# Block-sparse attention with an FFN on one core: the prologue's copies, banks and first matmuls rearranged

## The chip, the cores and the metric

The kernel runs on one core of a Trainium2 chip. The metric is the device time of one execution in microseconds (us), lower is better. The core has five engines with queues of their own that work in order: PE (matmul, with its weight loads shown apart as PEld), DVE, ACT, POOL, and SP, which here only issues DMAs. ACT issues a few DMAs too.

## The reference

```python
B, H, S, D = 4, 8, 768, 64; block = 32; n_blocks = 24
scores = q @ k.T / sqrt(D)
mask = |blk_i - blk_j| <= 1, or first/last block row or column, or kb in sampled_blocks[qb] (3 each)
scores = where(mask, scores, -1e9); scores -= scores.max(-1)
attn = exp(scores); attn /= attn.sum(-1) + 1e-9
x = (attn @ v) laid out as (B*S, 512)
h = x @ w_in                          # 512 -> 2048
g = where(h >= 1, h, where(h <= -1, 0, (h + 1)**2 / 4))
out = g @ w_out                       # 2048 -> 512
```

## The kernel before

The kernel goes through 32 pairs of batch and head. The eight heads of batch 0 are walked twice, half the queries (384) at a time, so that the first of two FFN passes can start early: 40 visits, of which the first is called head 0 here, the second head 1, and so on.

**A visit** has two parts. First come the row maxima: `max_mm` multiplies a 128-query slice with 384 keys (K = 88 rows: 64 of the head's dimension and 24 of the mask), `max_red` takes the maximum of that product on DVE, `max_col` joins two halves, `max_turn` transposes three columns into a row by PE with the identity `idr`, and `max_row` (ACT) writes the negative row into row 96 of the query operand. Then come the scores proper (K = 97, the extra row subtracts the maximum), `expo` on ACT, and the products with the values. A visit of batch 0's first pass has six `max_mm`, six score tiles and six exponentials.

**The mask** is carried by extra rows of the matmul. `ind` is a matrix of 38 rows and 768 columns from DRAM: 24 rows say to which block a column belongs, 8 are zero, 6 are one. It lands three times: in a scratch tile `raw` (called `early["ef"]` in the code), and in rows 64 to 101 of the two key tiles `KF[0]` and `KF[1]`. `mask()` makes a 24 by 24 table `mb` on DVE from the constants `cmt` and the sampled blocks `sraw`; `mask_half` multiplies it with the indicator on PE and copies the product into rows 64 to 87 of `QA[0]`; `mask_copies` spreads it to the other query tiles.

**Raw heads.** Heads 0 and 1 (`RAW`) are loaded into `KF`, `QF` (named KB, QB in rows of the trace) and used in full fp32 for the scores. `round_raw` casts them to fp32r into `KA0`, `QA0` (KA, QA; `KAt`, `QA` in the code) for the maxima.

**Order.** All steps lie in a list `plan` with a due time from tables of numbers (`P`, `PW`, ...); it is sorted once and written out, so every engine's order is fixed. `consts` (-100), `load_raw` of head 0 (-99), `consts_more` (-98), `mask` (-97) come first. DMAs take eight semaphores in turn, so an issue on SP waits until the DMA eight places before it has landed.

**PSUM.** `bank` hands out banks by rings of names: `RINGS["m"]` holds the three buffers of the pool `pa`, from which the first maxima and their transposes come; `RINGS["s"]` (`oa0`, `oa1`, `hp`) serves the scores.

Of the kernel before, what the change touches and what calls it, by code (L numbers as in the profile page):

```python
# [10 lines left out]
I32 = mybir.dt.int32  # L11
# [7 lines left out]
B, H, S, D = 4, 8, 768, 64  # L19
NB, BLK, NR = 24, 32, 3  # L20
T = 6
HALF = 384
# [5 lines left out]
KM = 64 + NB  # L28
KA = 96 + T
# [9 lines left out]
def body(ctx, tc, qk_t, v, sampled_blocks, moe_w_in, moe_w_out, ind, cm, ident, fold, out):  # L39
    nc = tc.nc  # L40
# [12 lines left out]
    cv = pool("cv", 1)  # L53
# [19 lines left out]
    def f(ap):  # L73
        return ap.bitcast(F32)
# [7 lines left out]
    QA = [cst.tile([128, S], F32R, name=f"QA{i}") for i in range(SETS)]  # L82
    KAt = [cst.tile([128, S], F32R, name=f"KA{i}") for i in range(SETS)]
# [3 lines left out]
    KF = [f(qk.tile([128, S], F32R, name="KB")) for i in range(2)]  # L87
    QF = [f(qk.tile([128, S], F32R, name="QB"))[:, 0:HALF] for i in range(2)]
    RAWS = len(KF)
# [7 lines left out]
    M = slice(64, KM)  # L97
    early = {}

    def consts():  # L100
        ef = early["ef"] = f(cv.tile([128, 1024, 2], I32, name="raw", bufs=2).rearrange("p c w -> p (c w)"))[64:KA, 0:S]
        nc.scalar.dma_start(out=ef, in_=ind)
        sraw = early["sraw"] = cst.tile([128, NR, 2], I32, name="sraw")
        nc.sync.dma_start(out=sraw[M], in_=sampled_blocks.bitcast(I32).rearrange("a (r w) -> a r w", w=2))
        cmt = early["cmt"] = cst.tile([128, 2 * NB], F32, name="cmt")
        nc.sync.dma_start(out=cmt[M], in_=cm)
        nc.vector.memset(eps, 1e-9)
        nc.vector.memset(half_c, 0.5)
        nc.scalar.copy(out=warm, in_=eps)
        nc.gpsimd.memset(f(QA[0][64:128]), 0.0)  # L110
        nc.gpsimd.memset(QF[0][64:128], 0.0)
        for i in range(1, ALL):
            nc.gpsimd.memset(f(QA[i][64:96]), 0.0)

    def consts_more():
        idf = early["idf"] = pp.tile([128, HALF], F32, name="pt")[:, 0:128]
        nc.sync.dma_start(out=idf, in_=ident)
        nc.vector.tensor_copy(out=KAt[0][64:KA], in_=early["ef"])
        nc.scalar.dma_start(out=KF[0][64:KA], in_=ind)
        rounded(nc.gpsimd, KAt[1][64:KA], early["ef"])  # L120

    def mask():
        sf = cst.tile([128, NR], F32, name="sf")
        nc.vector.tensor_copy(out=sf[M], in_=early["sraw"][M, :, 0])
        al = cst.tile([128, NB], F32, name="al")
        cmt = early["cmt"]
        nc.vector.tensor_copy(out=al[M], in_=cmt[M, 0:NB])
        for r in range(NR):
            nc.vector.scalar_tensor_tensor(
                out=al[M], in0=cmt[M, NB:2 * NB], scalar=sf[M, r:r + 1], in1=al[M],  # L130
                op0=ALU.is_equal, op1=ALU.max)
        mb = early["mb"] = cst.tile([128, NB], F32R, name="mb")
        nc.vector.tensor_scalar(out=mb[M], in0=al[M], scalar1=-1.0, scalar2=BIG, op0=ALU.add, op1=ALU.mult)
        mask_half(0, nc.vector)

    def mask_half(hf, eng):
        cs = slice(hf * HALF, (hf + 1) * HALF)
        pm = psa.tile([128, 512], F32, name="pa")
        nc.tensor.matmul(out=pm[0:NB, 0:HALF], lhsT=early["mb"][M], rhs=KAt[0][64:KM, cs], start=True, stop=True)
        rounded(eng, QA[0][64:KM, cs], pm[0:NB, 0:HALF])  # L140
        if hf == 0:
            nc.scalar.copy(out=QF[0][64:KM], in_=pm[0:NB, 0:HALF])

    def mask_copies():
        src = f(QA[0][64:KM, 0:HALF])
        rounded(nc.gpsimd, QA[1][64:KM, 0:HALF], src)
        nc.scalar.copy(out=idr, in_=early["idf"])
        for i in range(1, RAWS):
            nc.gpsimd.memset(QF[i][64:96], 0.0)
            nc.scalar.dma_start(out=KF[i][64:KA], in_=ind)  # L150
            rounded(nc.gpsimd, QF[i][64:KM], src)
        rounded(nc.gpsimd, KAt[2][64:KA], f(KAt[0][64:KA]))
        rounded(nc.gpsimd, QA[2][64:KM, 0:HALF], src)
        nc.sync.dma_start(out=sel, in_=fold)
        for i in range(3):
            nc.gpsimd.memset(PS[i], 0.0)
        nc.gpsimd.memset(ones, 1.0)
# [9 lines left out]
    def after(key, *needs):  # L167
        assert all(x in passed for x in needs), (key, needs)
        passed.add(key)
# [34 lines left out]
    def bank(wide, use="s"):  # L204

        if wide:
            ring = RINGS[use]
            n = turns[use] = turns.get(use, -1) + 1
            name = ring[n % len(ring)]
            if name[0] == "o":  # L210
                return psc.tile([128, DM], F32, name=name)
            if name == "hp":
                return psh.tile([128, 512], F32, name="hp")
        return psa.tile([128, 512], F32, name="pa")
# [47 lines left out]
    L, R = slice(0, 64), slice(64, 128)  # L262

    def rounded(eng, dst, src):
        if eng is nc.vector:
            eng.tensor_copy(out=dst, in_=src)
        elif eng is nc.gpsimd:
            eng.tensor_scalar(out=dst, in0=src, scalar1=1.0, scalar2=0.0, op0=ALU.mult, op1=ALU.add)
        else:
            eng.copy(out=dst, in_=src)  # L270

    def end_of(n):
        return ("S", n, 0 if n < H else 1, T - 1)

    def visit(n, n0, b, h, hfs, pst):

        j, e = divmod(h, 2)
        wide = n < H
        raw = n in RAW
        unit = len(hfs) == 1  # L280
# [3 lines left out]
        m = n % ALL if unit else (n + 1) % SETS  # L284
        QAi, KAi = QA[m], KAt[m]
        qs = slice(hfs[0] * HALF, (hfs[-1] + 1) * HALF)
        st = {}

        def free():
            m = n - (ALL if n <= 2 * H else SETS)  # L290
            return [] if m < 0 else [("red", m, TH - 1, 1)] if m in RAW else [end_of(m)]

# [5 lines left out]
        def round_raw():  # L298
            after(("A", n), ("raw", n), *free())
            rounded(nc.scalar, KAi[L], KF[n % RAWS][L])  # L300
            rounded(nc.scalar, QAi[L, qs], QF[n % RAWS][L])

        def load_direct():
            after(("ld", n), *([("B", n - 2)] if n - 2 in DIRECT else []))
# [79 lines left out]
        def max_mm(t, kh):  # L384
            after(("mm", n, t, kh), ("A", n))
            if "mc" not in st:
                st["mc"] = pr.tile([128, T, 2], F32, name="mc", bufs=2)
            pm = bank(wide, "m")
            nc.tensor.matmul(out=pm[:, 0:HALF], lhsT=QAi[0:KM, t * 128:(t + 1) * 128],  # L389
                             rhs=KAi[0:KM, kh * HALF:(kh + 1) * HALF], start=True, stop=True)  # L390
            st["pm", t, kh] = pm
# [11 lines left out]
        def max_turn(hf):  # L403
            after(("turn", n, hf), ("col", n))
            pm = st["pr", hf] = bank(wide, "m")
            for t in range(TH):
                nc.tensor.transpose(out=pm[0:1, t * 128:(t + 1) * 128].bitcast(F32R),  # L407
                                    in_=st["mr"][:, hf * TH + t - t0:hf * TH + t + 1 - t0], identity=idr)
# [7 lines left out]
        for m, (t, kh) in enumerate(jobs):  # L416
            u = n0 - (G["m0"] - G["m1"] * m / len(jobs))
            at(u, max_mm, t, kh)
            at(u + G["mr"], max_red, t, kh)
        at(n0 - G["mc"], max_col)  # L420
        for hf in hfs:
            at(n0 - G["mt"], max_turn, hf)
            at(n0 - G["mw"], max_row, hf)
# [104 lines left out]
        w = HALF * len(hfs)  # L528
# [33 lines left out]
        s = n0  # L562
# [160 lines left out]


    at(-100, consts)
    at(-98, consts_more)
    at(-97, mask)
    at(-PW["qs"] + 0.1, mask_copies)
    at(-PW["qs"] + 0.15, mask_rest)
    for n in range((B + 1) * H):  # L730
        if n < 2 * H:
            hf, h = divmod(n, H)
# [25 lines left out]
        traced(fn, *args)  # L758


RAW = range(2)
TOT = range(16)
LOPOOL = ()
# [18 lines left out]
PX = {'qs': 8.982, 'q2': 6.513, 'vs': 2.7, 'ld': 3.141, 'm0': 8.296, 'm1': 3.0, 'mr': 0.964, 'mc': 1.965, 'mt': 1.563, 'mw': 0.6, 'ex': 1.025, 'ps': 0.8, 'lag': 3.323, 'tt': 0.137, 'ot': 0.4, 'al': 0.627, 'su': 0.782, 'de': 1.067, 're': 4.161, 'r2': 2.821, 'xm': -2.273, 'xh': 0.956, 'xl': 1.844}  # L782
PA = {'q2': 5.823, 'qs': 8.343}
PM = {'gr': -0.448, 'gs': 0.124, 'gm': 0.164, 'gh': 0.294, 'gl': 2.955, 'l2': 1.529, 'l3': 0.148, 'l1': 0.116}
RINGS = {"s": ("oa0", "oa1", "hp"), "m": ("pa", "pa")}
DELAY = 7.661
SETS = 2
PER = 2 * T
# [8 lines left out]
def _constants():  # L797
    import numpy as np

    col = np.arange(S)  # L800
    block = (T * (col % 128) + col // 128) // BLK
    ind = np.concatenate([block[None, :] == np.arange(NB)[:, None], np.zeros((8, S)), np.ones((T, S))]).astype(np.float32)
    i, j = np.arange(NB)[:, None], np.arange(NB)[None, :]
    base = (abs(i - j) <= 1) | (i == 0) | (j == 0) | (i == NB - 1) | (j == NB - 1)
    cm = np.concatenate([base.astype(np.float32), np.broadcast_to(j, (NB, NB)).astype(np.float32)], axis=1)
    return {"ind": ind, "cm": np.ascontiguousarray(cm), "ident": np.eye(128, dtype=np.float32), "fold": np.tile(np.eye(32, dtype=np.float32), (4, 1))}
# [34 lines left out]
```

## Time and profile before

| | |
|---|---|
| median of 3 runs | 968.37 us (968.28 to 969.57) |
| the profiled execution, its own time | 967.62 us |
| its span | 965.8 us |
| PE busy | 939.0 us, 97% of the span |
| DVE, ACT, POOL busy | 529.3, 539.0, 261.6 us |
| mean granted clock of PE | 0.996 |

Times in rows are counted from the start of the span, which lies within the profiled execution's own time with 1.8 us around it. A busy PE is one on which a matmul is in flight; matmuls overlap by their pipeline, so the pace is read from the distance between starts, or from the chain of work, which gives each piece only the time that it adds.

### The profile page before, as it was taken

How to read it: one execution, taken by the hardware profiler on the slowest of the kernel's cores; microseconds unless marked ns; L12 is line 12 of the kernel's file. 1: busy time of each engine (PE TensorE's matmuls, PEld its weight loads, DVE VectorE, ACT ScalarE, POOL GpSimd, SP SyncE). 2: the span in 40 equal slices, each digit the busy share in tenths (PEclk: the TensorE clock that was granted, in tenths of full speed). 3: DMA queues.
4: the chain of work that ended last, by engine and by line, in shares of the span. 5: the costliest groups of instructions: out<-in, count | busy, mean ns of one | idle time of the engine just before them, and what ended most of it. 6: DMA issues, size and time to landing. Idle time of an engine off the chain costs nothing.

```text
span 965.8 us, 14030 instructions
## 1 busy us (share of the span) xinstructions
PE 939.0 (97%) x5018; PEld 768.7 (80%) x5018; DVE 529.3 (55%) x961; ACT 539.0 (56%) x1088; POOL 261.6 (27%) x260
## 2 busy tenths in 40 slices
PE   4989999999999999999999999999999999999998
PEld 2545577788888888788888888889888888999997
DVE  3899899866595556435545444455544343322222
ACT  3788787665765455544555454545545444433433
POOL 3000000354343445333443333334333333000000
PEclk9999999999999999999999999999999999999999
DMA  6466666678565655444445555554456423433442
GB/s 181 140 186 203 191 201 182 214 242 246 170 191 160 197 171 173 143 140 142 143 138 170 157 160 160 174 145 129 137 149 189 137 82 104 164 128 117 159 131 98
DMA packets 55941, 155.63 MB, mean 161 GB/s; under 512 B 9518, under 2 KB 17742, under 8 KB 55872
## 3 DMA queue, kind: packets, MB, share of 16 engines
q1 hardware_dynamic: 55688, 154.34, 51.9%
q8 instruction: 39, 0.64, 0.3%
q10 hardware_dynamic: 184, 0.40, 0.1%
q14 instruction: 30, 0.25, 0.1%
HBM read 110.00 MB, written 16.40 MB: 131 GB/s over the span
## 4 chain that ended last, share of the span: by engine, by line
PE 93%; ACT 3%; DMA 2%; DVE 1%; issue 0%; SPq 0%; ACTq 0%
PE po L461 12%; PE oa L667 9%; PE oa L668 9%; PE oa L669 9%; PE hp L633 9%; PE hp L634 8%; PE hp L635 8%; PE pa L389 7%; PE pa L432 6%; PE pa L433 6%; PE pa L635 1%; PE pa L634 1%; PE pa L633 1%; ACT pt L439 1%; PE pa L407 1%; PE oa L430 1%
## 5 line engine op out<-in xcount | busy, mean ns | idle before, releaser
L449 POOL TENSOR_TENSOR acc<-acc,pt 128x384 f32<-128x384 f32 x192 | 202.9, 1058 | 183.8 <-ACT pt L439 183.8
L395 DVE TENSOR_REDUCE mc<-pa 128x1 f32<-128x384 f32 x384 | 203.5, 552 | 49.4 <-PE pa L389 41.9
L439 ACT ACTIVATE pt<-pa 128x384 f32<-128x384 f32 x336 | 163.0, 488 | 101.3 <-PE pa L433 98.5
L648 DVE SCALAR_TENSOR_TENSOR r<-r,hp 128x384 f32<-128x384 f32 x112 | 61.1, 545 | 195.2 <-ACT r L644 195.1
L633 PE MATMUL hp<-x,wi 128*128 128x384 f32 x448 | 156.0, 348 | 0.9 <-DVE r L648 0.6
L667 PE MATMUL oa<-w,gh 128*128 128x512 f32 x384 | 151.6, 395 | 0.3 <-ACT gh L270 0.3
L634 PE MATMUL hp<-x,wi 128*128 128x384 f32 x448 | 151.7, 339 | 0.0
L635 PE MATMUL hp<-x,wi 128*128 128x384 f32 x448 | 151.4, 338 | 0.0
L668 PE MATMUL oa<-w,gh 128*128 128x512 f32 x384 | 151.4, 394 | 0.0
L669 PE MATMUL oa<-w,gl 128*128 128x512 f32 x384 | 151.3, 394 | 0.0
L449 POOL TENSOR_TENSOR acc<-pt 128x384 f32<-128x384 f32 x48 | 51.3, 1070 | 359.3 <-ACT pt L439 359.3
L461 PE MATMUL po<-pt,lv 128*64 128x384 f32 x720 | 126.0, 491 | 0.0
L389 PE MATMUL pa<-KA,QA 88*128 88x384 f32 x354 | 120.0, 360 | 4.0 <-ACT QA L270 1.5
L433 PE MATMUL pa<-QB,KB 128*128 128x384 f32 x336 | 114.0, 339 | 0.0
L432 PE MATMUL pa<-QA,KA 97*128 97x384 f32 x318 | 110.1, 346 | 1.9 <-ACT pt L439 1.0
L640 ACT ACTIVATE r<-hp,half_c 128x384 f32<-128x384 f32 x112 | 65.1, 581 | 81.3 <-PE hp L635 80.3
L270 ACT CAST gh<-r 128x384 fp32r<-128x384 f32 x128 | 65.7, 513 | 75.8 <-DVE r L648 75.7
L659 DVE TENSOR_TENSOR gl<-r,gh 128x384 fp32r<-128x384 f32 x128 | 72.6, 567 | 51.9 <-ACT gh L270 50.9
L461 PEld LDWEIGHTS po<-pt,lv 128*64 128x64 f32 x720 | 60.3, 137 | 48.7 <-issue 39.7
L633 PEld LDWEIGHTS hp<-x,wi 128*128 128x128 f32 x448 | 84.8, 189 | 17.2 <-issue 12.0
L634 PEld LDWEIGHTS hp<-x,wi 128*128 128x128 f32 x448 | 84.9, 190 | 2.2 <-issue 0.6
L669 PEld LDWEIGHTS oa<-w,gl 128*128 128x128 f32 x384 | 72.1, 188 | 16.1
(126 smaller groups left out, 1200.7 us busy)
## 6 DMA issues: line engine op xcount, KB each, us to landing
w<-wo_dram SPq DMA_DIRECT2D x112, 512.0 KB, 3.4
qk<-in_qk_t_dram SPq DMA_DIRECT2D x24, 384.0 KB, 3.7
raw<-in_moe_w_in_dram SPq DMA_DIRECT2D x16, 512.0 KB, 4.7
raw<-in_moe_w_out_dram SPq DMA_DIRECT2D x16, 512.0 KB, 4.4
wo_dram<-w SPq DMA_DIRECT2D x16, 512.0 KB, 3.6
lv<-in_v_dram SPq DMA_DIRECT2D x40, 192.0 KB, 2.8
out_dram<-o SPq DMA_DIRECT2D x7, 768.0 KB
KA<-qkh SPq DMA_DIRECT2D x24, 192.0 KB, 2.9
```

What stands on the lines that cost most here:

```text
L389: nc.tensor.matmul(out=pm[:, 0:HALF], lhsT=QAi[0:KM, t * 128:(t + 1) * 128], rhs=KAi[0:KM, kh * HALF:(kh + 1) * HALF], start=True, stop=True)
L395: nc.vector.reduce_max(out=st["mc"][:, t - t0, kh:kh + 1], in_=st.pop(("pm", t, kh))[:, 0:HALF], axis=AX.X)
L433: nc.tensor.matmul(out=ps[:, 0:HALF], lhsT=st["KB"][:, ks], rhs=st["QB"][:, cs], start=False, stop=True)
L439: nc.scalar.activation(out=p, in_=st.pop(("ps", hf, c))[:, 0:HALF], func=AF.Exp, scale=SCALE)
L449: nc.gpsimd.tensor_tensor(out=own["acc"][:, k], in0=prev, in1=st["p", hf, c], op=ALU.add)
L461: nc.tensor.matmul(out=st["po"][(L, R)[k], 0:HALF], lhsT=lv[k][:, c], rhs=p, start=(c == 0), stop=(c == T - 1))
L633: nc.tensor.matmul(out=hv, lhsT=wi[:, j, 0, fs], rhs=x[:, 0], start=(j == 0), stop=False)
L634: nc.tensor.matmul(out=hv, lhsT=wi[:, j, 0, fs], rhs=x[:, 1], start=False, stop=False)
L635: nc.tensor.matmul(out=hv, lhsT=wi[:, j, 1, fs], rhs=x[:, 0], start=False, stop=(j == NP - 1))
L667: nc.tensor.matmul(out=o, lhsT=gh[:, ts], rhs=w[:, 0], start=(fi == fis[0]), stop=False)
L668: nc.tensor.matmul(out=o, lhsT=gh[:, ts], rhs=w[:, 1], start=False, stop=False)
L669: nc.tensor.matmul(out=o, lhsT=gl[:, ts], rhs=w[:, 0], start=False, stop=(fi == fis[-1]))
```

## The change

It concerns what happens ahead of the first scores.

- The indicator gets 48 rows (16 of ones where there were 6); all three landings have 48 rows.
- The casts of the indicator into KA0 and KA1 both go to ACT (they were on DVE and POOL). The copy for head 2 (`KAt[2]`) reads `KF[1]`. `idr` is cast later in the program text.
- The first link of the mask's table reads `cmt` directly; a copy goes.
- The cast of head 0's queries moves from ACT to DVE; the mask's copy into `QF[0]` moves from ACT (out of PSUM) to POOL (out of `QA[0]`).
- The first six maxima take the banks pa, oa0, pa, oa1, pa, hp; their transposes' bank stays with pa.
- `keep_busy` issues matmuls whose products nobody reads: 20 ahead of the mask's product, 2 ahead of each of the first six `max_mm`, 12 ahead of the first transposes. Each writes into the bank that the real product then overwrites.

```diff
-        ef = early["ef"] = f(... name="raw" ...)[64:KA, 0:S]
+        ef = early["ef"] = f(... name="raw" ...)[64:112, 0:S]
...
-        nc.vector.tensor_copy(out=KAt[0][64:KA], in_=early["ef"])
-        nc.scalar.dma_start(out=KF[0][64:KA], in_=ind)
-        rounded(nc.gpsimd, KAt[1][64:KA], early["ef"])
+        for i in range(2):
+            rounded(nc.scalar, KAt[i][64:KA], early["ef"][0:KA - 64])
+        nc.scalar.dma_start(out=KF[0][64:112], in_=ind)
...
-        nc.vector.tensor_copy(out=al[M], in_=cmt[M, 0:NB])
...
-                out=al[M], in0=cmt[M, NB:2 * NB], scalar=sf[M, r:r + 1], in1=al[M],
+                out=al[M], in0=cmt[M, NB:2 * NB], scalar=sf[M, r:r + 1], in1=al[M] if r else cmt[M, 0:NB],
...
+    def keep_busy(out, k, x):
+        for _ in range(SPIN[k]):
+            nc.tensor.matmul(out=out[:, 0:HALF], lhsT=x[:, 0:128], rhs=x[:, 0:HALF], start=True, stop=True)
...
     def mask_half(hf, eng):
+        if hf == 0:
+            keep_busy(pm, 0, QA[0][64:128])
         nc.tensor.matmul(out=pm[0:NB, 0:HALF], lhsT=early["mb"][M], rhs=KAt[0][64:KM, cs], start=True, stop=True)
         rounded(eng, QA[0][64:KM, cs], pm[0:NB, 0:HALF])
-        if hf == 0:
-            nc.scalar.copy(out=QF[0][64:KM], in_=pm[0:NB, 0:HALF])
...
+        for i in range(RAWS):
+            if i:
+                nc.gpsimd.memset(QF[i][64:96], 0.0)
+                nc.scalar.dma_start(out=KF[i][64:112], in_=ind)
+            rounded(nc.gpsimd, QF[i][64:KM], src)
         nc.scalar.copy(out=idr, in_=early["idf"])
-        for i in range(1, RAWS):
-            nc.gpsimd.memset(QF[i][64:96], 0.0)
-            nc.scalar.dma_start(out=KF[i][64:KA], in_=ind)
-            rounded(nc.gpsimd, QF[i][64:KM], src)
-        rounded(nc.gpsimd, KAt[2][64:KA], f(KAt[0][64:KA]))
+        rounded(nc.gpsimd, KAt[2][64:KA], KF[1][64:KA])
...
-            rounded(nc.scalar, QAi[L, qs], QF[n % RAWS][L])
+            rounded(nc.scalar if n else nc.vector, QAi[L, qs], QF[n % RAWS][L])
...
-            pm = bank(wide, "m")
+            pm = bank(wide, "m" if n else "0")
+            if n == 0:
+                keep_busy(pm, 1, KAt[0][64:KM])
...
             pm = st["pr", hf] = bank(wide, "m")
+            if n == 0:
+                keep_busy(pm, 2, KAt[0][64:KM])
...
+SPIN = (20, 2, 12)
-RINGS = {"s": ("oa0", "oa1", "hp"), "m": ("pa", "pa")}
+RINGS = {"0": ("pa", "oa0", "pa", "oa1", "pa", "hp"), "s": ("oa0", "oa1", "hp"), "m": ("pa", "pa")}
-    ... np.zeros((8, S)), np.ones((T, S))])
+    ... np.zeros((8, S)), np.ones((16, S))])
```

On PE, from the program's start to the first transposes, before (L139 is the mask's product, L389 `max_mm`, L407 `max_turn`; KA0 and QA0 are head 0's operands, mb the mask's table):

```order
L139 MATMUL pa_160<-KA0_112,mb_158 24x384
L139 MATMUL pa_178<-KA0_112,mb_158 24x384
L389 MATMUL pa_184<-KA0_112,QA0_110 128x384
L389 MATMUL pa_186<-KA0_112,QA0_110 128x384
L389 MATMUL pa_188<-KA0_112,QA0_110 128x384
L389 MATMUL pa_190<-KA0_112,QA0_110 128x384
L389 MATMUL pa_192<-KA0_112,QA0_110 128x384
L389 MATMUL pa_194<-KA0_112,QA0_110 128x384
L407 MATMUL pa_208<-idr_105,mr_204 1x128 x3
```

And now (L137 is `keep_busy`, L144 the mask's product, L395 `max_mm`, L415 `max_turn`; between the rows shown and the last two, the fourth to sixth maximum stand in the same pattern of 2 and 1):

```order
L137 MATMUL pa_159<-QA0_110 128x384 x20
L144 MATMUL pa_159<-KA0_112,mb_157 24x384
L144 MATMUL pa_197<-KA0_112,mb_157 24x384
L137 MATMUL pa_203<-KA0_112 128x384 x2
L137 MATMUL oa0_207<-KA0_112 128x384 x2
L395 MATMUL pa_203<-KA0_112,QA0_110 128x384
L395 MATMUL oa0_207<-KA0_112,QA0_110 128x384
L137 MATMUL pa_211<-KA0_112 128x384 x2
L395 MATMUL pa_211<-KA0_112,QA0_110 128x384
...
L137 MATMUL pa_239<-KA0_112 128x384 x12
L415 MATMUL pa_239<-idr_105,mr_235 1x128 x3
```

Every real product kept its place; 44 fillers stand between them, the 20 first ones ahead of everything. Behind the transposes the order of PE is the old one to the end.

On ACT, from the program's start to the first `max_row`, before (L270 is `rounded`, L142 the copy in `mask_half`, L413 `max_row`):

```order
L119 DMA KB_116<-in_ind_dram 38x768
L150 DMA KB_117<-in_ind_dram 38x768
L270 CAST KA0_112<-KB_116 64x768
L142 COPY QB_118<-pa_160 24x384
L270 CAST QA0_110<-QB_118 64x384
L147 CAST idr_105<-pt_146 128x128
L270 CAST QA0_110<-pa_178 24x384
L270 CAST KA1_113<-KB_117 64x768
L270 CAST QA1_111<-QB_119 64x384
L270 CAST x_115<-qk_120 64x768
L270 CAST x_114<-qkh_122 64x384
L413 ACTIVATE QB_118<-pa_208 1x384
```

And now (L274 is `rounded`, L421 `max_row`):

```order
L120 DMA KB_116<-in_ind_dram 48x768
L274 CAST KA0_112<-raw_131 38x768
L274 CAST KA1_113<-raw_131 38x768
L274 CAST KA0_112<-KB_116 64x768
L153 DMA KB_117<-in_ind_dram 48x768
L155 CAST idr_105<-pt_146 128x128
L274 CAST QA0_110<-pa_197 24x384
L274 CAST KA1_113<-KB_117 64x768
L274 CAST QA1_111<-QB_119 64x384
L274 CAST x_115<-qk_120 64x768
L274 CAST x_114<-qkh_122 64x384
L421 ACTIVATE QB_118<-pa_239 1x384
```

Two casts came in ahead of head 0's key cast, the mask's copy and the query cast went out behind it, and the third load of the indicator is now issued behind the key cast. The casts of heads 1 and 2 still stand ahead of the first `max_row`. In head 0's exponentials one pair is swapped: the cast QA0<-qkh stands behind the second exponential, where it stood behind the third.

## Rows read from the trace of the kernel before

**Rows 1.** The page's first lines: the span, then busy time, share of the span and instructions of each engine.

```profile
span 965.8 us, 14030 instructions
PE 939.0 (97%) x5018; PEld 768.7 (80%) x5018; DVE 529.3 (55%) x961; ACT 539.0 (56%) x1088; POOL 261.6 (27%) x260
```

**Rows 2.** Busy time of each engine in three stretches, cut where the first scores start (17.41), where head 1's first scores start (27.02) and at 45.36. Columns: stretch, length, busy time with the number of instructions for PE, PEld, DVE, ACT, POOL, then the granted clock, the share of the DMA engines and GB/s.

```profile
0.00:17.41 17.41, 5.01 (x13) 2.50 (x14) 6.94 (x19) 6.91 (x12) 7.57 (x20) 1.00 0.52 142
17.41:27.02 9.61, 9.11 (x21) 5.51 (x21) 2.84 (x7) 4.55 (x10) 0.00 (x0) 1.00 0.59 198
27.02:45.36 18.34, 16.46 (x91) 8.60 (x91) 17.38 (x28) 14.45 (x28) 0.00 (x0) 1.00 0.61 173
```

**Rows 3.** The chain of work that ended last, in order of time, its first 60 us: start, time that the piece adds, what.

```profile
2.19 6.86 DMA QB<-in_qk_t_dram
9.07 6.52 DMA qk<-in_qk_t_dram
15.61 1.24 ACT x L270 x2
16.88 0.49 ACT QB L413
17.41 1.65 PE oa L430 x2
...
20.02 1.28 PE oa L430 x2
...
25.30 0.66 PE hp L430 x2
...
47.23 0.32 PE hp L433
...
52.17 0.18 PE hp L433
```

**Rows 4.** The timeline of the DMA issues: start, length of the issue, queue, line, what is loaded. (SP's issue at 6.14 waited for the indicator in `raw`.)

```profile
0.74 0.43 SPq L104 DMA_DIRECT2D sraw<-in_sampled_blocks_dram  x1
0.74 0.55 ACTq L102 DMA_DIRECT2D raw<-in_ind_dram  x1
1.23 0.32 SPq L106 DMA_DIRECT2D cmt<-in_cm_dram  x1
6.14 0.47 SPq L295 DMA_DIRECT2D KB<-in_qk_t_dram  x1
17.02 1.38 SPq L235 DMA_DIRECT2D raw<-in_moe_w_in_dram  x3
```

**Rows 5.** Single microseconds near the start, columns as in rows 2; the last two are the busy share of the 16 DMA engines and GB/s.

```profile
3.00:4.00 1.00, 0.00 (x0) 0.00 (x0) 0.07 (x1) 0.00 (x0) 0.92 (x6) 1.00 0.82 269
5.00:6.00 1.00, 0.00 (x0) 0.00 (x0) 0.00 (x0) 0.00 (x0) 0.00 (x0) 1.00 0.13 50
6.00:7.00 1.00, 0.00 (x0) 0.00 (x0) 0.66 (x1) 0.00 (x0) 0.71 (x1) 1.00 0.12 49
```

**Rows 6.** The timeline from the first memset to the first transposes: start, busy time, engine, line, what, and in brackets the idle time before and what ended it.

```profile
0.73 0.73 POOL L110 MEMSET QA<- 64x768 f32 x1 [0.29 <-POOLq L821]
3.93 0.16 DVE L124 CAST sf<-sraw 24x3 f32<-24x3 int32 x1 [3.03 <-DMA sraw<-in_sampled_blocks_dram]
6.34 0.81 DVE L127 COPY al<-cmt 24x24 f32<-24x24 f32 x1 [2.25 <-DMA cmt<-in_cm_dram]
7.18 0.23 DVE L129 SCALAR_TENSOR_TENSOR al<-cmt,sf,al 24x24 f32<-24x24 f32 x1
7.81 0.83 ACT L270 CAST KA<-KB 64x768 fp32r<-64x768 f32 x1 [5.00 <-DMA KB<-in_qk_t_dram]
8.34 0.17 DVE L133 TENSOR_SCALAR mb<-al 24x24 fp32r<-24x24 f32 x1
8.57 0.83 PE L139 MATMUL pa<-KA,mb 24*24 24x384 f32 x2 [8.57 <-DVE mb L133]
9.19 0.55 DVE L266 CAST QA<-pa 24x384 fp32r<-24x384 f32 x1 [0.68 <-PE pa L139]
10.89 2.96 PE L389 MATMUL pa<-KA,QA 88*128 88x384 f32 x6 [1.49 <-ACT QA L270]
11.61 2.88 DVE L395 TENSOR_REDUCE mc<-pa 128x1 f32<-128x384 f32 x6 [1.87 <-PE pa L389]
14.74 0.48 PE L407 MATMUL pa<-idr,mr 128*1 128x128 f32 x3 [0.90 <-DVE mr L401]
```

**Rows 7.** The timeline of ACT in head 0 (an exponential and a cast), and the first step of converting the FFN's weights that landed from the issue at 17.02.

```profile
19.09 0.49 ACT L439 ACTIVATE pt<-oa 128x384 f32<-128x384 f32 x1 [1.74 <-PE oa L430]
19.48 0.82 ACT L270 CAST KA<-acc 64x768 fp32r<-64x768 f32 x1
23.32 0.50 ACT L270 CAST QA<-qkh 64x384 fp32r<-64x384 f32 x1
29.54 1.12 ACT L242 ACTIVATE cva<-raw 128x1024 f32<-128x1024 f32 x1
```

**Rows 8.** Single microseconds around 45, columns as in rows 2; the granted clock is the third number from the end.

```profile
44.00:45.00 1.00, 0.59 (x5) 0.27 (x2) 1.00 (x2) 0.97 (x3) 0.00 (x0) 1.00 0.48 184
46.00:47.00 1.00, 1.00 (x4) 1.00 (x4) 0.31 (x1) 0.96 (x2) 0.00 (x0) 0.50 0.04 6
49.00:50.00 1.00, 1.00 (x4) 0.41 (x6) 1.00 (x3) 1.00 (x3) 0.00 (x0) 1.00 0.49 154
```

More of the change, by code (lines that the diff above doesn't have):

```diff
@@ L100, in consts @@
     def consts():
-        ef = early["ef"] = f(cv.tile([128, 1024, 2], I32, name="raw", bufs=2).rearrange("p c w -> p (c w)"))[64:KA, 0:S]
+        ef = early["ef"] = f(cv.tile([128, 1024, 2], I32, name="raw", bufs=2).rearrange("p c w -> p (c w)"))[64:112, 0:S]
         nc.scalar.dma_start(out=ef, in_=ind)
@@ L801, in _constants @@
     block = (T * (col % 128) + col // 128) // BLK
-    ind = np.concatenate([block[None, :] == np.arange(NB)[:, None], np.zeros((8, S)), np.ones((T, S))]).astype(np.float32)
+    ind = np.concatenate([block[None, :] == np.arange(NB)[:, None], np.zeros((8, S)), np.ones((16, S))]).astype(np.float32)
     i, j = np.arange(NB)[:, None], np.arange(NB)[None, :]
```

## The prediction, made before the changed kernel had run

> **What bounds the kernel now.** I read the page's first lines, then busy time by stretch, then the chain of work, then the timeline of the start. PE is in flight for 97% of the span [rows 1], and the 26.8 us in which it is not lie mostly in front: until the first scores at 17.41 it is busy for 5.0 us [rows 2]. So whatever shortens the start should move the whole rest forward, unless something in the rest is pinned to another clock.
>
> A busy PE is not a fast one there. A score product of a raw head adds 1.28 us to the chain at 20.02 and 0.66 at 25.30; a single product of 384 columns adds 0.32 at 47.23 and 0.18 at 52.17 [rows 3]. Around 45 the granted clock goes from 1.00 to 0.50 and back [rows 8]: these are the levels of 1.2 and 2.4 GHz. The clock column reads 1.00 from the start, but by the durations PE is at the lower level until about 25. So head 0, from 17.41 to 27.02, is PE-bound at half speed.
>
> Ahead of it the chain is one of loads and of ACT's order: head 0's queries land at 9.05, SP then issues the load for head 2, which lands at 15.6, ACT casts it (1.24 us), and only behind these casts stands the first `max_row` at 16.88 [rows 3], though its transposes had ended at 15.22 [rows 6]. The loads are slow: between 5 and 7 us 0.12 to 0.13 of the DMA engines are busy, two of sixteen, after 0.82 between 3 and 4 [rows 5]. The indicator of 38 rows is what still runs then; SP's next issue waits for it until 6.14 [rows 4].
>
> **The loads.** If 48 rows spread over all engines, what is asked for at the start (two indicators of 147 KB, 192 and 96 KB of head 0, 64 KB of identity, about 650 KB) takes 2.4 us at the 269 GB/s of rows 5, so all has landed by about 5.5. The smallest load, `sraw`, takes 3.2 us (0.74 to 3.93, [rows 4, 6]); by that the indicator in `raw` is there at 4.0 to 4.5. The other end is no gain, if 48 rows use as few engines; I take the spread, since the loads of 64 rows beside it did keep 0.82 of the engines busy. The Trainium skill ("DMA: Bandwidth & Descriptors", section on why a DMA increments its semaphore by 16) says that a DMA uses the largest number of engines up to 16 that divides its rows: 2 for 38, 16 for 48. By that rule the spread is certain; the two busy engines of rows 5 agree, and no row here shows 48 rows.
>
> **The mask's table.** `cmt` was used at 6.34; issued at 1.23, it should be there at about 4.4 like `sraw`. The copy of 0.81 us goes; three links of 0.23 and the last step of 0.17 remain, so `mb` is ready at about 5.4 instead of 8.5 [rows 6]. ACT's two indicator casts cost at most 0.83 each, as head 0's key cast did [rows 6]: from 4.3 to 6.0, and the key cast to 6.8. The query cast on DVE (bounded by nothing and that 0.83) lies ahead of the mask's product: hidden.
>
> **The fillers.** They begin when the memset of QA ends, at 1.46 [rows 6]. At 0.32 each, 20 last 6.4 us, to 7.9. When does the clock rise? In head 0 it was still low at 20.02 and full at 25.30, up to 7.9 us after work resumed at 17.41 [rows 3]; after the fall at 45 it was back within 3 to 5 us [rows 8]. So it rises between 4.5 and 9.4; I take 6.5, in the middle, where 15.6 fillers are done and 4.4 remain at 0.18: end at 7.3 (bounds 6.4 and 7.9). The mask's product, ready at about 5.5, thus waits for its fillers. Then, as before, 0.62 us to DVE's copy and 0.55 for it [rows 6], and no ACT cast behind it: the first maximum starts at 8.5 (7.6 to 9.1) instead of 10.89.
>
> **Maxima and transposes.** With six banks PE runs on without waiting for DVE. From the first maximum to the last are 14 products (6 real, 8 fillers; the first four fillers lie beside DVE's copy), 2.5 us at 0.18, then 12 fillers, 2.2 us: 13.2. DVE's own way is shorter: 0.72 from the first product to the first maximum, 2.88 for six, 0.25 to the transposes [rows 6], 12.35. The last fillers therefore hold the transposes back by 0.85 us, the visible price of this part. Transposes 0.48, row 0.49 and a step of 0.04 make the first scores start at 14.2. ACT must by then have cast head 2's load: at the latest, landing 6.52 us after 5.5 as before, and 1.24 of casts [rows 3], it is free at 13.3, just before `max_row` needs it at 13.7. The gain up to here is 17.41 - 14.2 = 3.2 us (2.3 to 4.1).
>
> **Head 0 at full clock.** It took 9.61 us [rows 2]. PE then needs six score products of 0.66, four maxima of 0.18 and the transposes, 5.2 us. ACT needs six exponentials of 0.49, casts of 0.82 and 0.50 [rows 7] and a row of 0.49, 4.75 us, beginning about 0.9 us after the first score starts (half of the 1.68 from 17.41 to 19.09): 5.65. With two small waits I take 6.0, a gain of 3.6 (3.0 to 3.95).
>
> **Edits costed at nothing.** POOL's copy into `QF[0]`, at the 0.55 us of DVE's copy of that shape [rows 6], follows another such copy behind the mask's, is done near 9.6 and lies beside the maxima; uncovered it would cost its 0.55. The third indicator, issued at about 7, lands near 10 and is wanted by head 1 and head 2's copy, near 20. The swap of a cast and an exponential changes ACT's order by 0.50 us where both are due.
>
> **Does the rest follow?** From 27.02 to 45.36 DVE is busy for 17.38 of 18.34 us [rows 2], so the gain would stop there if DVE's work hung on something fixed. Its first conversion step follows ACT's at 29.54 [rows 7], on weights issued at 17.02 [rows 4]. Moved by 6.8 us, ACT wants them at 22.7; three loads of 512 KB at 269 GB/s need 5.8 us, so even unmoved they would land at about 22.8, and SP's queue begins its second round about 2 us earlier. It follows.
>
> **The sum.** 3.2 + 3.6 = 6.8 us off the profiled execution's 967.62 makes 960.8. That execution lies 0.75 below the median of the runs, so the forecast is 961.6.
>
> **The rivals.** *The fillers do not lift the clock, or too late* (slower): PE at half speed has 20 fillers to 7.9, the mask's products 0.64, four fillers 1.28, 14 products 4.5, 12 fillers 3.8, transposes and row 1.0: first scores at 19.2, 1.8 us later than before, 970.2. This needs the rise after about 14.5, since each us of that work run at full speed gives back a half; against it stand both rises seen, for it that the 20 first ones use 64 rows, and zeros.
>
> *The clock falls back in head 0* (smaller gain): between transposes and scores PE idles about half a us, and the three score banks make it wait for exponentials, as in the stretch before the fall at 45, with PE busy for 0.59 of a us [rows 8]. Only the 3.2 remain: 965.2. The Trainium skill ("TensorE: Matmul & The Clock Gate", section on depth-cycling of the PSUM queue) describes this: small pauses of a PE that cycles through banks let the clock go up and down. The trace shows it once, at 45, while from 25 to 44 the same cycling kept the clock full.
>
> *The indicator is no faster:* the first scores stay at 17.41 behind head 2's casts, and head 0 alone gains: 964.8.
>
> *More than forecast:* the fall at 45 costs about half of the 3 to 5 us that it lasts, 1.5 to 2.5; shifted, PE may miss it: about 959.6. *No change* would need the rest to be pinned after all: 968.4.
>
> **How the numbers follow.** Chances: forecast 0.52 (its own range 960.3 to 963.1), more 0.14, the two smaller gains 0.21, no lift 0.09, no change 0.04. The range reaches down to where the missed fall adds to the best ends of both terms, 960.3 - 2.5 = 957.8, and up to 965.6, which takes in the smaller gains. Within 0.2%, 1.9 us, a measurement of this kernel can hardly tell a change. Faster by more: 0.52 + 0.14 + 0.20 = 0.86; slower by more: about half of no lift, 0.05; the rest, 0.09, within.
>
> **What would show it.** Right: the indicator landed by 4.5; key cast on ACT before 7; mask's product right behind the fillers at about 7.3; first scores near 14.2, head 1's near 20.2, score products 0.66 apart; later rows earlier by about 6.8. Wrong: `max_row` still waiting behind ACT's casts, score products 1.3 apart, or PE waiting longer between 20 and 40 than it did from 27 to 45.

## The result, and the profile after

The changed kernel takes 978.42 us (median of 12 runs, 971.25 to 983.55) where the kernel before took 969.35 beside it on the same chip: ratio 1.0087, 95% interval 1.0062 to 1.0113. (The ratios here and below are those on record; the quotient of two medians differs from them by up to 0.2%.) It is slower by 9.1 us; 961.6 was forecast.

The profiled execution of the changed kernel took 979.20 us. Its page begins as follows (beside [rows 1]):

```profile
span 977.4 us, 14123 instructions
PE 959.6 (98%) x5062; PEld 783.4 (80%) x5062; DVE 530.3 (54%) x960; ACT 540.2 (55%) x1088; POOL 261.8 (27%) x260
```

PE is in flight for 20.6 us more, DVE, ACT and POOL for at most 1.2: the loss is on PE. The loads did what was forecast. This is the timeline of SP, ACT and DVE around the indicator's landing (beside [rows 4, 6]: start, length, engine, line, what, idle time before):

```profile
3.78 1.56 ACT L274 CAST KA<-raw 38x768 fp32r<-38x768 f32 x2 [1.11 <-DMA raw<-in_ind_dram]
4.29 0.47 SPq L299 DMA_DIRECT2D KB<-in_qk_t_dram  x1
4.96 0.17 DVE L132 TENSOR_SCALAR mb<-al 24x24 fp32r<-24x24 f32 x1
5.36 0.83 ACT L274 CAST KA<-KB 64x768 fp32r<-64x768 f32 x1
```

The indicator is there at 3.8, and SP's issue that waited for it until 6.14 goes out at 4.29. The mask's table is ready at 5.13 instead of 8.5. All that the first products need is there about 3 us earlier. PE takes none of it. Its timeline to head 1's first scores (L137 fillers, L144 the mask's product, L395 the first maxima, L415 transposes, L438 scores):

```profile
1.52 6.76 PE L137 MATMUL pa<-QA 64*128 64x384 f32 x20 [1.52 <-POOL QA L110]
8.21 0.83 PE L144 MATMUL pa<-KA,mb 24*24 24x384 f32 x2
...
12.12 0.69 PE L395 MATMUL pa<-KA,QA 88*128 88x384 f32 x1
12.74 1.00 PE L137 MATMUL oa<-KA 24*128 24x384 f32 x2
13.68 0.69 PE L395 MATMUL oa<-KA,QA 88*128 88x384 f32 x1
...
17.40 4.20 PE L137 MATMUL pa<-KA 24*128 24x384 f32 x12
21.54 0.48 PE L415 MATMUL pa<-idr,mr 128*1 128x128 f32 x3
...
22.70 1.62 PE L438 MATMUL oa<-QB,KB 97*128 97x384 f32 x2
...
32.20 0.91 PE L438 MATMUL oa<-QB,KB 97*128 97x384 f32 x2 [0.50 <-ACT QB L421]
```

Twenty fillers from 1.52 to the mask's product at 8.21 are 0.33 us each, the pace of 1.2 GHz (0.32 for 384 columns, [rows 3]), and so are the twelve from 17.40 to 21.54 (0.34 each). PE worked almost without a gap for 20 us, and the clock did not rise. Between them a step of one maximum and two fillers takes 1.55 us (12.12 to 13.68), where three products at that pace make 0.96. The first scores start at 22.70, 5.29 later than before; head 0 then runs at half speed as it used to, 9.50 us where it took 9.61 [rows 2].

The rest shows in busy time by stretch (columns as in rows 2, the granted clock third from the end; in the first stretch it reads 1.00 while the distances between starts tell half speed):

```profile
22.70:32.20 9.50, 9.00 (x22) 5.41 (x22) 3.65 (x9) 4.56 (x10) 0.00 (x0) 1.00 0.00 0
50.00:55.00 5.00, 3.95 (x12) 3.60 (x12) 3.73 (x9) 3.93 (x8) 0.00 (x0) 0.56 0.35 98
...
70.00:75.00 5.00, 4.79 (x18) 3.53 (x20) 4.62 (x10) 4.41 (x10) 0.00 (x0) 0.66 0.60 193
...
110.00:115.00 5.00, 4.60 (x16) 2.41 (x17) 3.23 (x6) 3.19 (x7) 0.00 (x0) 0.50 0.35 103
```

After head 1 the clock falls three times (near 51, 71 and 109) where it fell once before 120 us in the kernel before [rows 8]. Transposes are later than before by 5.2 at head 1, by 6.7 behind the first fall, by about 7.5 behind the second, by 9.4 to 10 behind the third, and by 11.7 at the last visit; the growth after the third fall comes with no fall on record. Part of that is this execution: its mean clock is 0.990, the mean of the 12 runs is 0.9939 and that of 61 runs of the kernel before 0.9952 (one more, at 0.945, is left out), and a line through the times and clocks of all runs, with a level for each kernel, has a slope of 0.66 us per 0.001. By that line, 7.3 us remain at equal clock.

### The profile page after: what moved, and what is told of

The parts are those of the page before. It is cut to its first block, busy times and chain, and to the rows that moved or that the text cites. A ratio compares the mean times of both kernels' runs of the same rounds, so it can differ in the third digit from the quotient of the medians.

```text
span 977.4 us, 14123 instructions
## 1 busy us (share of the span) xinstructions
PE 959.6 (98%) x5062; PEld 783.4 (80%) x5062; DVE 530.3 (54%) x960; ACT 540.2 (55%) x1088; POOL 261.8 (27%) x260
## 4 chain that ended last, share of the span: by engine, by line
PE 87%; DVE 4%; DMA 4%; ACT 3%; issue 1%; SPq 0%; POOL 0%; ACTq 0%; POOLq 0%; DVEq 0%
PE po L469 11%; PE oa L675 8%; PE oa L676 8%; PE oa L677 8%; PE hp L641 8%; PE hp L642 7%; PE hp L643 7%; PE pa L395 6%; PE pa L440 6%; PE pa L441 5%; PE pa L137 1%; ACT pt L447 1%; PE pa L643 1%; PE pa L642 1%; PE pa L641 1%; DVE mc L401 1%
## 5 line engine op out<-in xcount | busy, mean ns | idle before, releaser
L395 PE MATMUL pa<-KA,QA 88*128 88x384 f32 x351 | 119.9, 361 | 3.6 <-DVE mc L401 1.4
L274 ACT CAST gh<-r 128x384 fp32r<-128x384 f32 x128 | 65.7, 513 | 77.3 <-DVE r L656 77.1
```

## The experiments

**Are the fillers the loss? (e1, e2)** My theory after the result: everything ahead of the fillers gained what was forecast, and the fillers, which do not lift the clock, cost all of it and more. The rival: something else in the rebuilt start (ACT's new order, the banks) is slower.

```diff
-SPIN = (20, 2, 12)
+SPIN = (0, 0, 0)      # e1
+SPIN = (20, 0, 0)     # e2
```

> The changed kernel with no filler matmuls at all (SPIN 0, 0, 0); everything else of the change stays. Theory A, that the fillers run at the low clock, never lift it, and simply stand in PE's way: the mask's product starts at about 5.3 (its table was ready at 5.13 in the changed kernel), the first maximum at about 6.8, the transposes at about 10.7, and the first scores at 11.5 to 12.5, when ACT is through with the casts of head 2, against 22.70 with fillers and 17.41 before. Head 0 still at half speed, 9.6 us. The time is then 5 to 6 us below the kernel before, about 963 to 964, ratio 0.994. Theory B, that the loss comes later, from the clock that falls three times between 50 and 116 instead of once, because the prologue's new order shifts the stages against each other: the first scores come early all the same, but the falls stay, and the time is no better than the kernel before, 968 to 974.

Measured: 964.18 against 968.57, ratio 0.9942 (0.9921 to 0.9963). PE in e1:

```profile
5.13 0.80 PE L144 MATMUL pa<-KA,mb 24*24 24x384 f32 x2 [5.13 <-DVE mb L132]
...
10.79 0.48 PE L415 MATMUL pa<-idr,mr 128*1 128x128 f32 x3 [1.60 <-DVE mr L407]
...
12.31 1.62 PE L438 MATMUL oa<-QB,KB 97*128 97x384 f32 x2 [0.29 <-issue]
```

The mask's product follows the table at 5.13, the first scores start 5.1 earlier than before, and head 0 takes 10.2 us at half speed; head 1 starts at 22.50, 4.5 earlier than before. Without the fillers the change is a gain of 4.4 us. In the changed kernel they moved the first scores from 12.31 to 22.70. (Some casts, exponentials and loads of the first heads stand in another order on ACT and SP in e1 than in the changed kernel; e4 below has the changed kernel's order.)

> The changed kernel with the first 20 fillers alone (SPIN 20, 0, 0). Theory A: these end at 8.28 as in the changed kernel, the first maximum starts at about 9.6, six maxima on DVE at 0.48 each end at about 13.2, the transposes at about 13.9, first scores at 14.5: 8 us earlier than with all fillers, 3 us earlier than the kernel before, and 3 us later than without any. The time lies about 3 us below the kernel before. If the fillers between the maxima and ahead of the transposes were harmless, the first scores would stay near 22.

Measured: 967.61, ratio 0.9991 (0.9975 to 1.0008); first scores at 14.62 as expected, the time 2 us above the expected one. The first 20 fillers cost 2.3 us of the 10.4 at the first scores; the other 24 cost 8.1.

**Why does the clock not rise? (e3, e5, e6)** The first 20 fillers multiply 64 rows of zeros. The same 20, on other operands (diff shortened, numbers put in):

```diff
+        nc.vector.memset(f(wi[0:128, 0, 0, 0:HALF]), 1.0)    # e3; 0.0 in e5; wi[64:128], 1.0 in e6
...
-            keep_busy(pm, 0, QA[0][64:128])
+            keep_busy(pm, 0, wi[0:128, 0, 0])                # wi[64:128, 0, 0] in e6
...
-SPIN = (20, 2, 12)
+SPIN = (20, 0, 0)
```

> As the run with the first 20 fillers alone, but each filler multiplies 128 rows of ones (a corner of the weights' tile, set by a memset on DVE) where the changed kernel's first 20 multiply 64 rows of zeros. Theory C, that the clock answers to how much of the array works, not to PE being busy: the clock rises while the 20 fillers run or soon behind them, products of 384 columns then start 0.16 to 0.18 apart, the first scores come at about 13, head 0 takes 6 us instead of 9.6, and the time is 7 to 8 us below the kernel before. Theory D, that fillers of this length at the start never lift the clock, whatever they multiply: as the run with the first 20 alone, score products 1.28 apart until about 22.

> The changed kernel with the first 20 fillers alone, each over 128 rows of zeros. With 128 rows of ones the 20 fillers lasted 5.30 us (the clock rose within them), with 64 rows of zeros 6.76. Theory C1, that the number of rows decides: 5.3 to 5.7 us, the mask's product at about 6.6, maxima 0.18 apart. Theory C2, that zeros do not count: 6.7 us as with 64 rows of zeros, the mask's product at about 8.2, maxima 0.32 apart.

> The same with 64 rows (partitions 64 to 127) of ones. Theory C1 (rows decide): about 6.7 us, no rise, maxima 0.32 apart. Theory C2 (zeros do not count, any ones do): 5.3 to 5.7 us, maxima 0.18 apart. If both this and the 128 rows of zeros stay slow, rows and data both count.

PE in e3 (128 rows of ones):

```profile
1.35 5.30 PE L138 MATMUL pa<-wi 128*128 128x384 f32 x20 [1.35 <-DVE half_c L109]
...
7.98 0.34 PE L396 MATMUL oa<-KA,QA 88*128 88x384 f32 x1
8.15 0.34 PE L396 MATMUL pa<-KA,QA 88*128 88x384 f32 x1
...
11.66 0.48 PE L416 MATMUL pa<-idr,mr 128*1 128x128 f32 x3 [2.43 <-ACT x L275]
...
12.82 1.62 PE L439 MATMUL oa<-QB,KB 97*128 97x384 f32 x2
```

Its stretch from these transposes to the next (columns as in rows 2):

```profile
11.66:21.34 9.68, 9.68 (x21) 5.93 (x22) 3.23 (x7) 4.01 (x8) 0.42 (x1) 0.50 0.64 187
```

In e5 (128 rows of zeros), and then in e6 (64 rows of ones):

```profile
1.35 5.20 PE L138 MATMUL pa<-wi 128*128 128x384 f32 x20 [1.35 <-DVE half_c L109]
```

```profile
1.43 6.77 PE L138 MATMUL pa<-wi 64*128 64x384 f32 x20 [1.43 <-DVE wi L108]
...
9.90 0.53 PE L396 MATMUL oa<-KA,QA 88*128 88x384 f32 x1
10.22 0.53 PE L396 MATMUL pa<-KA,QA 88*128 88x384 f32 x1
```

With 128 rows the 20 fillers take 5.2 to 5.3 us and the maxima behind them stand 0.17 apart: the clock rose to 2.4 GHz on the way, with zeros as with ones. With 64 rows, zeros (e2) or ones (e6), they take 6.8 and the maxima stand 0.32 apart. In these runs the number of rows made the difference, not the values. In e3 PE then idles for 2.43 us ahead of the transposes, and by 11.66 it is back at half speed, this time with a granted clock of 0.50 on record; head 0 takes 10.3 us, so the 6 us expected for it were missed, and the time is 965.64, ratio 0.9971 (0.9946 to 0.9997). e5 took 966.48 and e6 964.12 in one execution each beside 967.94; their mean clocks (0.987 and 1.000) differ by more falls further on, so those two times say nothing about the start.

**All fillers with 128 rows (e4).** The diff of e3 with `SPIN = (20, 2, 12)` as in the changed kernel, and the same operands in groups 1 and 2.

> All 44 fillers of the change, each with 128 rows of ones. Theory C: the clock rises by about 8 and stays up; a filler and its step cost about 0.18, the first scores come near 14.2 as the prediction worked out, head 1's near 20.2, and the time is about 6.8 us below the kernel before. Theory D: first scores near 22.7 and the time about that of the changed kernel.

Measured: 964.48, ratio 0.9955 (0.9932 to 0.9977). PE in e4, then the stretch of head 0:

```profile
8.87 0.34 PE L396 MATMUL pa<-KA,QA 88*128 88x384 f32 x1
9.05 0.51 PE L138 MATMUL oa<-wi 128*128 128x384 f32 x2
9.40 0.34 PE L396 MATMUL oa<-KA,QA 88*128 88x384 f32 x1
...
10.63 2.27 PE L138 MATMUL pa<-wi 128*128 128x384 f32 x12
12.74 0.34 PE L416 MATMUL pa<-idr,mr 128*1 128x128 f32 x3
...
13.77 0.88 PE L439 MATMUL oa<-QB,KB 97*128 97x384 f32 x2 [0.28 <-issue]
...
19.67 0.91 PE L439 MATMUL oa<-QB,KB 97*128 97x384 f32 x2 [0.51 <-ACT QB L422]
```

```profile
13.77:19.67 5.90, 5.39 (x22) 3.37 (x22) 3.36 (x9) 4.47 (x10) 0.00 (x0) 1.00 0.85 303
```

This is the start that the prediction worked out: first scores at 13.77 (14.2), head 0 in 5.90 (6.0), head 1 at 19.67 (20.2). In the traces e4 differs from the changed kernel in what the fillers multiply, in the memset of that on DVE, and in nothing else of the order of any engine. So what the fillers multiply makes the way from 9.1 us above the kernel before to 4.1 below it. Yet the time is no better than e1's. Transposes are 7.35 earlier than before from head 1 to head 3, and 5.30 at head 4. The 2 us are lost here, on ACT and then on PE:

```profile
34.42 1.07 ACTq L514 DMA_DIRECT2D s<-acc  x1
```

```profile
38.50 0.44 PE L441 MATMUL oa<-QA,KA 97*128 97x384 f32 x1 [1.22 <-ACT QA L422]
...
40.25 0.18 DVE L524 SCALAR_TENSOR_TENSOR rc<-rt 24x32 f32<-24x32 f32 x1 [1.30 <-DMA rt<-s]
...
41.85 0.91 PE L396 MATMUL pa<-KA,QA 88*128 88x384 f32 x2 [1.09 <-DVE mc L402]
```

```profile
41.00:42.00 1.00, 0.15 (x1) 0.15 (x1) 0.97 (x4) 1.00 (x3) 0.00 (x0) 1.00 0.76 188
...
44.00:45.00 1.00, 1.00 (x4) 0.24 (x2) 1.00 (x4) 0.00 (x0) 0.00 (x0) 0.50 0.78 254
```

The first store of `s1` holds ACT's queue for 1.07 us instead of 0.58. PE then waits 1.22 us for ACT's row at 38.50 and 1.09 for DVE's maximum at 41.85, so that it works for 0.15 us between 41 and 42; from 43 to 46 it runs at half speed. The kernel before had its fall there too [rows 8], so this one is no new cost by itself. The waits are: from head 3's transposes to head 4's PE idles for 2.32 us. In the kernel before it idled for 0.77 there, all of it for the same row. The store's 0.5 is a part of ACT's. DVE's maximum is late because DVE, in its order, first waited 1.30 us for the load `rt`, which brings back what `s1` stored (0.90 in the kernel before, 0.78 in e9).

**What does a change of rows cost? (e8)** In the changed kernel the fillers of groups 1 and 2 multiply rows 64 to 87 and the maxima rows 0 to 87. In e8 both use 0 to 87:

```diff
-                keep_busy(pm, 1, KAt[0][64:KM])
+                keep_busy(pm, 1, KAt[0][0:KM])     # and in group 2
```

> The changed kernel with its first 20 fillers as they are (64 rows of zeros), but the 2 ahead of each maximum and the 12 ahead of the transposes take the 88 rows that the maxima themselves use, instead of the 24 rows of the indicator. In the changed kernel a step of two fillers and a maximum takes 1.55 us at the low clock, of which three products are 0.96. Theory G, that the weights of a product that uses other rows than the one before cannot be loaded ahead, so each change of rows costs about 0.3: a step then takes 0.96, the maxima end 3 us earlier, first scores at about 19.5. Theory C1: 88 rows of real data may also lift the clock, as the 97 rows of head 0 do, after about 8 us of them: then the last fillers take 0.18 each. If a step still takes 1.55, something else than the rows makes it.

PE in e8:

```profile
9.77 0.52 PE L395 MATMUL pa<-KA,QA 88*128 88x384 f32 x1
10.09 0.84 PE L137 MATMUL oa<-KA 88*128 88x384 f32 x2
10.73 0.52 PE L395 MATMUL oa<-KA,QA 88*128 88x384 f32 x1
...
14.89 4.04 PE L137 MATMUL pa<-KA 88*128 88x384 f32 x12
18.73 0.52 PE L415 MATMUL pa<-idr,mr 128*1 128x128 f32 x3
19.93 1.62 PE L438 MATMUL oa<-QB,KB 97*128 97x384 f32 x2
```

The step is 0.96 us, three products at 0.32, and the first scores start at 19.93: the changes of rows cost 2.8 of the 22.70. The clock did not rise here either, in 10 us of products of 88 rows. (Head 0's own products of 97 rows were followed by a rise in every run where the clock was low, in e8 at about 26.4. They are of fp32 and take 0.64 us each at half speed, so 88 rows against 97 is no test of the rows alone.) One execution took 967.86. The weight loads of the changed kernel show the price:

```profile
13.67 0.29 PEld L395 LDWEIGHTS oa<-KA,QA 88*128 88x128 f32 x1 [0.44 <-issue]
14.29 0.50 PEld L137 LDWEIGHTS pa<-KA 24*128 24x128 f32 x2 [0.33 <-issue]
```

A load behind a product of other rows starts only when that product has passed (0.33 to 0.44 us of idle of the load engine), so its own 0.28 to 0.29 us lie bare, twice in a step; in e8 and e4 loads lie beside the product ahead (in e8 one from 9.78 beside the product from 9.77).

**Is the indicator the gain? (e7)** The kernel before, with the three landings of the indicator in 48 rows and nothing else (diff shortened).

```diff
-    ... np.zeros((8, S)), np.ones((T, S))])
+    ... np.zeros((8, S)), np.ones((16, S))])
-        nc.scalar.dma_start(out=KF[0][64:KA], in_=ind)
+        nc.scalar.dma_start(out=KF[0][64:112], in_=ind)     # and in raw and KF[i]
```

> The kernel before with the indicator in 48 rows, and nothing else of the change. Theory E, that the loads spread over all engines and the start hangs on them: the indicator lands at about 3.8 instead of 6.1, head 0's keys at 5.3 instead of 7.8, the first maximum starts at about 8.3 instead of 10.9, first scores at about 13 instead of 17.41, and the time is about 4 us below the kernel before (ratio 0.996), most of what the change without fillers gives (12.31). Theory F, that the other rearrangements of the change (casts, banks, the mask's table) make most of the gain: first scores at 15 to 17, 1 to 2 us below.

Measured: 965.22 against 967.94, ratio 0.9955 (0.9931 to 0.9979); first scores at 13.33 and head 1 at 23.18, within 1.0 and 0.7 us of e1. The rows of the indicator are most of the gain; the other edits of the start add 0.7 us at head 1, which the times of e1 and e7 cannot tell apart.

**Fewer of them (e9), and ACT's store (e10, e11).** e9 is e4 with `SPIN = (15, 2, 8)`: e4's 20 ended at 6.91, 1.8 us behind the table, and its 12 held the transposes until 12.74. (In the traces e9 also has e1's order of ACT and SP in the first heads and not e4's, so it is not the number of fillers alone.) e10 is e9, and e11 the kernel before, with one more line:

```diff
-    Q_S1 = nc.scalar
+    Q_S1 = nc.sync
```

> The changed kernel with 128 rows of ones in all fillers, as in e4, and fewer of them: 15 ahead of the mask's product, 2 ahead of each first maximum, 8 ahead of the transposes. Theory H (what the clock needs is that PE works through until head 0's scores with products that use all rows, and e4 had more of that than was needed): the 15 end near 6.1 instead of 6.9, the mask's product follows at once, first maximum near 7.4, transposes near 11.6, first scores near 12.7, head 0 again in 6.0 us and head 1 near 18.7, 1 us before e4's 19.67; time 1 us below e4's, about 5 to 6 below the kernel before (ratio near 0.994). Rival: eight fillers leave PE idle ahead of the transposes and the clock falls back as in e3; then head 0 takes 10 us, head 1 begins near 22.8, and the time is 1 to 2 us above e4's.

> e9 with one more edit: the stores of `s1` are issued by SP's queue instead of ACT's, where the first of the eight takes 1.07 us in e1, e4 and the changed kernel and 0.58 in the kernel before. Theory P (this issue, and ACT's delay from it, is what sets off PE's waits and the fall of the clock behind head 3 in e4): the shift of all rows against the kernel before stays near what it is at head 1 until behind head 3, and the time is 1.5 to 2.5 us below e9's. Rival Q (the fall comes from three score banks and DVE's load there, not from the issue): ACT gains 0.5 to 1 us there and the time stays within 1 us of e9's. Rival R (the store waits in SP's queue and holds loads behind it): 1 us or more above e9.

> The kernel before with only that edit, the stores of `s1` on SP's queue. It shows what the edit is worth by itself: theory P 0.5 to 1 us less, with the fall of the clock around 45 shorter or gone (up to 2.5 us less); rival Q no difference that can be measured; rival R slower by 1 us or more, with waits for loads issued by SP.

e9 measured 962.21 against 968.16, ratio 0.9923 (0.9901 to 0.9945). PE in e9, and a later stretch:

```profile
11.47 0.34 PE L416 MATMUL pa<-idr,mr 128*1 128x128 f32 x3 [0.15 <-DVE mr L408]
...
12.49 0.88 PE L439 MATMUL oa<-QB,KB 97*128 97x384 f32 x2 [0.27 <-issue]
...
18.38 0.91 PE L439 MATMUL oa<-QB,KB 97*128 97x384 f32 x2 [0.51 <-ACT QB L422]
```

```profile
40.00:45.00 5.00, 4.43 (x23) 2.28 (x23) 4.96 (x11) 3.87 (x8) 0.00 (x0) 1.00 0.77 210
```

First scores at 12.49, head 0 in 5.89, head 1 8.64 earlier than before, and in this execution, the fastest of six, 8.3 are still there at the end: it has no fall around 40, though ACT's store took 1.06 there too. It is the fastest kernel of this study, by 6 us against the kernel before and some 15 against the changed one, each taken with the kernel before beside it. Against e1, which has no fillers, head 1 starts 4.1 us earlier in the trace; the times are 2 us apart, and the two intervals overlap.

e10 took 965.47 (ratio 0.9961, 0.9941 to 0.9980) and e11 972.35 (ratio 1.0040, 1.0023 to 1.0057), 3.3 and 4.2 us above the same kernel without the line. But the line changes more than a queue. In the traces PE, DVE, ACT and SP have their work in another order from head 3 on, so the order that is written out does not come from the due times alone. Ahead of head 11's transposes PE has done 10 of the FFN's first products where e9 and the kernel before have done 18, and from there to head 12's it does 19 instead of 9. The transposes lose 5.4 us between these two heads, but in part that is work that moved. At head 15 all four kernels have done the same number; from head 9 to there e11 has lost 4.2 us against the kernel before and e10 3.6 against e9. In both the clock falls once in between; in e11:

```profile
119.95 0.69 PE L432 MATMUL pa<-x 97*128 97x384 f32 x1 [0.71 <-ACT pt L439]
```

```profile
120.00:121.00 1.00, 1.00 (x3) 1.00 (x4) 0.94 (x3) 1.00 (x3) 0.00 (x0) 0.50 0.64 194
```

PE waited 0.71 us there for an exponential, with none of the FFN's products in between, where the kernel before has some, and then ran at half speed until 123.4. Half speed over 3.4 us costs at most 1.7, so the clock is less than half of the loss. The fall around 45 is still there in e11 (a granted clock of 0.67 from 45 to 50). What theory P forecast did not come. What the store's queue is worth at an unchanged order, these two runs do not show, and they do not settle Q and R.

## Why the prediction was wrong, point by point

- **The loads and the table: right.** Indicator at 3.8 (4.0 to 4.5 was said), key cast on ACT from 5.36 to 6.19 (before 7), table at 5.13 (5.4). By the medians the 48 rows alone are worth 2.7 us (e7), the whole start without fillers 4.4 (e1); by the ratios 4.4 and 5.6.
- **"So it rises between 4.5 and 9.4; I take 6.5": the step that failed.** Both bounds were taken from rises under score products of 97 and 128 rows [rows 3, 8] and put on fillers of 64 and 24. (The middle of the two is 6.95 and not 6.5, which would move the sum by 0.2 us.) With 64 rows it did not rise in 6.8 us (e6: whatever the values), with 24 and 88 rows mixed not up to head 0, with 88 not from 8.97 to 18.73 (e8); with 128 it rose within 5.3 (e3, e5). The prediction had the clue ("64 rows, and zeros") and gave it a chance of 0.09; the rows made the difference, the zeros did not. The Trainium skill ("TensorE: Matmul & The Clock Gate", Part 1) says that sustained matmul activity lifts the clock, and says nothing there of rows; the products of 128 rows here agree, and those of 64 and 88, 0.32 apart without a gap, do not.
- **The rival "no lift" was 3.5 us short at the first scores** (19.2 said, 22.70 measured) and 8 at the end (970.2 and 978.42). It priced every filler at 0.32, which is e8's case (19.93). That fillers of other rows lay bare the weight loads, 2.8 us, stood in no step.
- **"ACT is free at 13.3, just before `max_row` needs it": the right neighbour.** In e1 the transposes ended at 11.27 and `max_row` started at 11.73, right behind these casts: whoever takes the fillers away meets them next. In e3 the profile puts the 2.43 us that PE waited ahead of the transposes down to the same casts, which ended at 11.54; but DVE's last step of the maxima, which the transposes read, ended at 11.52, so that wait may as well be DVE's.
- **"Head 0 at full clock, 6.0": right where the clock is full** (5.90 in e4, 5.89 in e9), wrong in the changed kernel (9.50), by the step above.
- **"It follows": half right.** DVE and the FFN's weights do not pin the rest: of e9's 8.64 us at head 1, 8.3 are there at the end. But e9's profile has no fall of the clock at all where the kernel before has two (near 45 and 390), so some of its gain went on the way and came back there. And the prediction let the fall at 45 only go or stay. In e4, 2 of 7.35 us went with the waits of ACT's row and DVE's maximum, beside a fall as before; in the changed kernel's profile the three falls lie where the 5.2 at head 1 grow to 9.4, and the rest up to 11.7 comes later, from a cause that no run shows.

The sum thus comes out as: loads and edits, 4.5 us earlier at head 1 (e1); fillers, 9.7 later there (22.50 to 32.20); together the 5.2 of the trace; and about 2 more at equal clock (7.3), which stay unexplained. Which of the falls of the clock a shift of all work brings is not settled. They differ between executions of one kernel: the 12 of the changed kernel have mean clocks from 0.990 to 1.000 and times from 983.55 down to 971.25. And the same wait does not always bring one: PE waits 1.22 us for head 3's row in e1, e2, e3, e5, e7 and the changed kernel, where the fall comes within 0.5 us of the wait's end; in e4, where it comes 4.5 us later; and in e6, e8 and e9, where none follows.

## What to carry to other kernels

A matmul put in to hold PE's clock should be tested for its pace in the trace: the distance between starts tells the level, where the granted clock reads 1.00 from the start all the same. Here fillers of 128 rows raised it and those of 64, 24 and 88 did not. Let the fillers end when the first real operand is ready (with e9's 15 and 8 the first scores came 1.3 us earlier than with e4's 20 and 12), and look at the waits that follow: in e3 the clock was lost again in one of 2.43 us. Before rows of one stretch are used as bounds for another, compare their shapes. And before a run of one changed line is read, compare the order of the engines' work in the two traces (e10, e11).

## What the runs showed of the hardware

- 20 products of 64 rows (e2, e6) and 30 of 88 (e8) at a steady 0.32 us were not followed by a rise of PE's clock; among 20 of 128 rows the distance went from 0.32 to 0.18, with zeros too (e3, e5).
- Consecutive products of different row ranges (64 to 87, then 0 to 87) left weight loads uncovered, 0.28 to 0.29 us each; equal ranges, or 128 rows beside 88 (e4: 0.53 us for three products), did not. The Trainium skill ("TensorE: Matmul & The Clock Gate", Part 3, what overlaps and what doesn't) lists that weight loads overlap products in flight only when their row groups differ; just before, it names a load into a background weight buffer as another way. The traces here show loads of equal rows beside the product, and the wait where the rows differ but overlap.
- 48 rows instead of 38 brought the indicator from 6.1 to 3.8 us. The Trainium skill's rule that the prediction names ("DMA: Bandwidth & Descriptors": 16 engines for 48 rows, 2 for 38) agrees with the busy share of the engines: 0.96 and 0.92 from 3 to 5 us, while these loads ran, where the kernel before had 0.13 and 0.12 from 5 to 7 with 38 rows still on the way [rows 5].
- The issue of one kind of store, that of `s1`, took ACT's queue 0.48 to 1.07 us: the first of them 0.58 in the kernel before and 1.06 to 1.07 in e1, e4, e7, e9 and the changed kernel, later ones 0.48 to 0.51.
